# Attention and a mixture of experts on one core: the experts' split weights get two sets of buffers, the short block a second full stationary tile, and the planner a new table

## The chip, the cores and the metric

The kernel runs on one core of a Trainium2 chip. The metric is the device time of one execution in microseconds. Engines are called TensorE (PE; its weight loads are PEld), VectorE (DVE), ScalarE (ACT), GpSimd (POOL) and SyncE (SP, which issues DMAs); the DMA engines move data beside them. L1709 is line 1709 of the kernel before.

## The reference

The first part is attention with pooled queries over 8 batches and 8 heads of 1152 x 64; its output is laid out as 4608 tokens of 512 numbers. The second part is a mixture of 8 experts with a fixed capacity of 576 tokens each:

```python
logits = x @ w_gate                      # (4608, 8)
order = np.argsort(-logits.flatten())    # best pair of token and expert first
for idx in order:
    tok, e = idx // E, idx % E
    if assigned[tok] >= 0 or counts[e] >= cap: continue
    assigned[tok] = e; counts[e] += 1
    ...
for e in range(E):
    mask = assigned == e
    h = np.maximum(x[mask] @ w1[e], 0.0)   # w1[e] is 512 x 1024
    out[mask] = h @ w2[e]                  # w2[e] is 1024 x 512
```

## The kernel before, in words

Attention comes first. Its order of instructions is written out in a table of its own (class `Timed`, table `TIME`), and the change leaves that table alone. Behind it stands `experts`, which handles the eight experts in turn, in the order in which they fill up. For an expert k three functions add operations to one list:

- `route(k, ...)` finds by a search in rounds (L1282 to L1311, VectorE with small matmuls L1288 and L1297) which expert fills up next and which tokens it gets; its result is the table of indices `idx[k]`. The next expert's routing needs this one's result.
- `fetch(k, ...)` loads the raw 32-bit weights W1 and W2 (L1563, indirect DMAs from GpSimd's queue) and the rows of x (XG, L1568). For the first two experts TensorE transposes x (`by_pe`, L1509 to L1518); for the others VectorE transposes squares of 32 and SP moves them into place with 16 DMAs (`by_dve`, L1528, L1535), then ScalarE and GpSimd split them (L1547, L1549, L1553). All matmuls work on 16-bit floats: each operand is split into a high half (rounded) and a low half (what the rounding left). So that the halves keep their range, the weights are scaled by a power of two, which comes from the sum of their squares: ScalarE squares W1 (L1587, tag `wq`) and W2 (L1609, tag `vq`) in four pieces each, small matmuls of one moving column add up the partitions (L1596, tag `ws`, and L1615, tag `vt`), and VectorE makes the scale (L1600, L1619). Then 16 pieces of the weights are split (tags `wh` and `vh` for the high halves on ScalarE, `wl` and `vl` for the low ones on GpSimd, L1663). For nearly all pieces ScalarE does a pair of operations: it scales the 32-bit piece in place (L1653) and copies it to the 16-bit high half (L1657); GpSimd then subtracts the high half from the scaled piece.
- `ffn(k, ...)` does the two products. The first (L1679, tag `mm`): 8 blocks of 128 hidden columns in two parts of 256 and 320 tokens, 12 matmuls each into PSUM tiles `ph`. Of each part ScalarE makes a pair (tag `re`): Relu in place in PSUM (L1684), then a copy to the high half HH (L1685); VectorE subtracts to get the low half HL (L1689, L1691). HH and HL lie side by side in one tile HX. The second product (L1709, tag `m2`): 5 blocks of tokens into `po`, four of 128 tokens and a short one of 64. A full block takes 24 matmuls of 512 moving columns, three for each of 8 pieces z: HH with W2H, HH with W2L, HL with W2H. The short block takes 16: one whose 128 stationary columns are the 64 of HH and the 64 of HL together, with W2H (L1706), and one whose stationary columns are the 64 of HH alone, with W2L. ScalarE takes a block out of PSUM (L1714, or L1717 and VectorE's L1719 for the short one) and GpSimd scatters it to the output (L1724, function `put`).

What sets the order: `Order.emit` is a planner in the program that builds the kernel. It knows for each operation the engine, a duration in ns (the number behind the engine's name in `od.add`), what it reads and writes by keys, and costs of handing over between engines (`EOWN`, `EWAIT`, and `switch` for TensorE between small and large matmuls). It plays the list through; where several operations of an engine are ready it takes the one with the smallest `(-first, t + lead)`, t being 10 per expert and a little more for later stages, `lead` coming from the table ELEAD by tag. From ELATE comes a delay in ns by which an operation's users are held back in the plan. The kernel's instructions are then issued in the planned order; each engine works its own list in that order and waits at an instruction until what it needs is there. The keys of the halves, `("W1H", z, y)` and so on, are the same for all experts, as there is one set of buffers W1h, W1l, W2H, W2L (and one of the raw weights W1, W2): an expert's halves can be written only when the matmuls of the expert before that read that piece are done.

Of the kernel before, what the change touches and what calls it, by code (L numbers as in the profile page):

```python
# [51 lines left out]
class Order:  # L52
# [15 lines left out]
    def add(self, t, eng, dur, fn, r=(), w=(), late=0, first=0, tag=None, kind=0, lock=None, k=None):  # L68
# [5 lines left out]
        late = late + self.late.get(tag, 0)  # L74
        pri = t + self.lead.get(tag, 0) + (self.lead.get(f"{tag}.{k}", 0) if k is not None else 0)
# [492 lines left out]
def attention(ctx, tc, top, kb, sx, kt, qt, v, wg, x_dram, L, npair=NPAIR):  # L568
# [483 lines left out]
    for n in range(1, npair, 2):  # L1052
# [8 lines left out]
        else:  # L1061
# [16 lines left out]
ELEAD = {"ar": 4.9, "be": 51.6, "bo": 2.8, "cl": 28.5, "cmp": 29.1, "dv": 1.5, "dw": -46.1, "dx": -41.8,  # L1078
# [5 lines left out]
ELATE = {"ar": -300, "bo": -300, "cl": -300, "cmp": 150, "dv": 1900, "dw": 750, "dx": 1500, "fa": -150, "fl": -300,  # L1084
# [4 lines left out]


def experts(ctx, tc, top, kb, sx, x_dram, L, w1, w2, out, C):
# [91 lines left out]
    W1h, W1l = one([128, 4, F], F16, "W1h"), one([128, 4, F], F16, "W1l")  # L1183
# [6 lines left out]
    W2H, W2L = one([128, 8, DM], F16, "W2H"), one([128, 8, DM], F16, "W2L")  # L1190
# [331 lines left out]
    def by_dve(k, t):  # L1522
# [8 lines left out]
        for s in range(4):  # L1531
# [14 lines left out]
            def high(src=src, cols=cols):  # L1546
                nc.scalar.activation(src, src, AF.Copy, scale=xs)  # L1547
                for o, c in cols(Xh):
                    nc.scalar.copy(o, src[:, :, c])  # L1549
# [240 lines left out]
```

## Time and profile before

| | us |
|---|---|
| median of the runs (lowest to highest of 3) | 1340.38 (1337.77 to 1343.58) |
| the profiled execution | 1334.67 |
| its span in the trace | 1332.9 |
| TensorE busy in the span (matmuls) | 1244.5 (93%) |
| VectorE | 1052.7 (79%) |
| ScalarE | 993.6 (75%) |
| GpSimd | 761.6 (57%) |

The page of the profile also gives the busy share of each engine in 40 slices of the span:

```profile
PE   7899999999999999999999997789899999999796
DVE  8999999999999999999999966888786777643020
ACT  4578777877887777787787660679887888897681
POOL 5275566656657556665665660365575565656351
PEclk7799999999999999999999998989999999999898
DMA  5755764665666566476465400442543534333301
```

Each digit is the busy share of a slice of 33.3 us in tenths; PEclk is the clock granted to TensorE in tenths of full speed. The experts begin near the 25th slice. Matmuls are pipelined: a matmul's duration holds the time until its result is out, so starts of neighbours, not durations, tell what one costs.

### The profile page before, as it was taken

Reading aid. Unit: us, or ns where it says so; the run is one execution under the profiler, and the core shown is the slowest. Engines: PE = TensorE matmul, PEld = TensorE weight load, DVE = VectorE, ACT = ScalarE, POOL = GpSimd, SP = SyncE. Lnnn points to the kernel's source line nnn. Section 1 sums busy time; section 2 is a strip of 40 time slices with the busy share of each in tenths; the row PEclk is TensorE's granted clock in tenths of the full one; section 3 lists DMA queues with packets and bytes.
Section 4 is the critical chain, followed back from the end, with each engine's and each line's share of the span. In section 5 each row is a group of like instructions: output and inputs, shape, how many; then the busy total and the mean of one; then the engine's idle time right before and its main releaser. Section 6 shows DMA issues by size and latency. Waiting matters only on the chain.

```text
span 1332.9 us, 39667 instructions
## 1 busy us (share of the span) xinstructions
PE 1244.5 (93%) x15483; PEld 884.1 (66%) x15483; DVE 1052.7 (79%) x2662; ACT 993.6 (75%) x2299; POOL 761.6 (57%) x757
## 2 busy tenths in 40 slices
PE   7899999999999999999999997789899999999796
PEld 4577787778778777777777775555554646556362
DVE  8999999999999999999999966888786777643020
ACT  4578777877887777787787660679887888897681
POOL 5275566656657556665665660365575565656351
PEclk7799999999999999999999998989999999999898
DMA  5755764665666566476465400442543534333301
GB/s 156 172 144 131 173 165 119 170 155 128 166 151 156 130 159 161 117 187 158 113 172 132 107 15 19 163 169 90 154 134 107 197 103 147 123 127 119 116 21 36
DMA packets 123545, 175.29 MB, mean 132 GB/s; under 512 B 49500, under 2 KB 86364, under 8 KB 121180
## 3 DMA queue, kind: packets, MB, share of 16 engines
q1 hardware_dynamic: 114876, 120.29, 35.6%
q0 software_dynamic: 8336, 52.44, 11.4%
q8 instruction: 121, 1.98, 0.7%
q14 instruction: 68, 0.56, 0.1%
q10 hardware_dynamic: 144, 0.02, 0.0%
HBM read 99.63 MB, written 18.87 MB: 89 GB/s over the span
## 4 chain that ended last, share of the span: by engine, by line
PE 58%; DVE 15%; ACT 13%; issue 7%; DMA 4%; SPq 1%; POOL 1%; ACTq 0%; POOLq 0%; DVEq 0%
PE av L890 16%; PE mt L770 9%; PE sc L873 6%; PE po L1709 6%; PE sc L874 5%; PE ph L1679 5%; DVE MX L797 4%; ACT W L1653 3%; PE kb L873 3%; PE kb L874 3%; DVE PM L880 2%; ACT WQ L1609 2%; DMA XG<-XB 1%; ACT W2H L1657 1%; ACT HX L1685 1%
## 5 line engine op out<-in xcount | busy, mean ns | idle before, releaser
L880 POOL TENSOR_TENSOR PM<-P 128x576 f16<-128x576 f32 x413 | 474.0, 1175 | 312.8 <-ACT P L877 263.0
L797 DVE TENSOR_REDUCE MX<-mt 128x2 f32<-128x768 f32 (+1 forms) x443 | 399.4, 921 | 39.6 <-PE mt L770 36.5
L877 ACT ACTIVATE P<-sc 128x288 f32<-128x288 f32 x768 | 296.5, 413 | 139.2 <-PE sc L874 127.6
L890 PEld LDWEIGHTS <-P 128*128 128x128 bf16 x5760 | 297.2, 98 | 28.1 <-issue 1.3
L890 PE MATMUL av<-V,P 128*128 128x65 f16 (+1 forms) x5760 | 305.8, 193 | 0.0
L890 PE MATMUL av<-V,PM 128*128 128x65 f16 x2880 | 296.4, 195 | 0.0
L890 PEld LDWEIGHTS <-PM 128*128 128x128 f16 x2880 | 265.4, 97 | 0.0
L874 PE MATMUL sc<-QB,KB 66*128 66x288 f16 (+1 forms) x768 | 216.7, 288 | 2.0 <-DMA QB<-AU 1.4
L873 PE MATMUL sc<-QA,KA 128*128 128x288 f16 x768 | 215.4, 286 | 1.7 <-ACT P L877 1.4
L770 PE MATMUL mt<-KH,BD 128*128 128x384 f16 x837 | 200.6, 326 | 10.4 <-DVE MX L797 4.5
L877 ACT ACTIVATE P<-kb 128x288 f32<-128x288 f32 x384 | 158.2, 412 | 32.9 <-PE kb L874 31.4
L1709 PE MATMUL po<-W2H,HX 128*128 128x512 f16 x512 | 165.8, 392 | 3.5 <-ACT OT L1714 3.5
L1709 PEld LDWEIGHTS <-HX 128*128 128x128 f16 (+1 forms) x832 | 77.5, 100 | 112.7 <-issue 46.7
L1679 PE MATMUL ph<-Xh,W1h 128*128 128x320 f16 (+1 forms) x512 | 147.9, 289 | 2.7 <-ACT Xh L1516 1.5
L874 PEld LDWEIGHTS <-KB 66*128 66x128 f16 (+1 forms) x1152 | 112.1, 97 | 56.3 <-issue 16.9
L1679 PE MATMUL ph<-Xl,W1h 128*128 128x320 f16 (+1 forms) x512 | 147.8, 289 | 0.6 <-DVE Xl L1518 0.6
L1679 PE MATMUL ph<-Xh,W1l 128*128 128x320 f16 (+1 forms) x512 | 147.8, 289 | 0.0
L873 PEld LDWEIGHTS <-KA 128*128 128x128 f16 x1152 | 112.9, 98 | 49.6 <-issue 15.8
L880 DVE TENSOR_TENSOR PM<-P 128x576 f16<-128x576 f32 x163 | 127.7, 793 | 6.8 <-ACT P L877 5.8
L1709 PE MATMUL po<-W2L,HX 128*128 128x512 f16 (+1 forms) x320 | 126.4, 395 | 0.0
L1663 POOL TENSOR_TENSOR W1l<-W,W1h 128x512 f16<-128x512 f32 x62 | 71.7, 1157 | 93.7 <-ACT W1h L1657 58.8
L1679 PEld LDWEIGHTS <-W1h 128*128 128x128 f16 x1024 | 99.9, 99 | 32.8 <-issue 5.7
(271 smaller groups left out, 2174.1 us busy)
## 6 DMA issues: line engine op xcount, KB each, us to landing
QD<-in_qt_dram SPq DMA_DIRECT2D x32, 576.0 KB
KD<-in_kt_dram SPq DMA_DIRECT2D x64, 288.0 KB
VD<-in_v_dram SPq DMA_DIRECT2D x32, 576.0 KB
QA<-QH SPq DMA_DIRECT2D x128, 72.0 KB
KA<-KH SPq DMA_DIRECT2D x64, 144.0 KB
KB<-KH SPq DMA_DIRECT2D x64, 144.0 KB
KA<-KL SPq DMA_DIRECT2D x64, 144.0 KB
x_dram<-X SPq DMA_DIRECT2D x16, 576.0 KB
```

The lines of the kernel that those rows point to most:

```text
L770: nc.tensor.matmul(out, BD[i][:, j], KH[i][:, ks], start=True, stop=True)
L797: od.add(t, "DVE", d, lambda: nc.vector.tensor_reduce(dst, src, axis=AX.X, op=OP.max), r=[mk], w=[("MX", i, j, c) for j, c in what], tag=" ...
L873: nc.tensor.matmul(c[:, :288], KA[i][:, s, ks], QA[i][:, s, qs], start=True, stop=False)
L874: nc.tensor.matmul(c[:, :288], KB[i][:kr, s, ks], QB[i][:kr, s, qs], start=False, stop=True)
L877: od.add(g + 0.1 + 0.01 * t, "ACT", 293, lambda c=c, qs=qs: nc.scalar.activation(p[:, qs], c[:, :288], AF.Exp, scale=1.0 / UNIT), r=[ck], ...
L880: od.add(g + 0.2, en, dur, lock=1, fn=lambda: eng.tensor_tensor(pm, p, hi, op=OP.subtract), r=[("P32", g % NP, 0), ("P32", g % NP, 1)], w= ...
L890: nc.tensor.matmul(out, w[:, qs], v, start=kb == 0 and j == 0 and y == 0, stop=kb == NKB - 1 and y == 2, skip_group_check=True)
L1609: od.add(t + 0.5, "ACT", 960, lambda z=z: nc.scalar.activation(WQ, W2.rearrange("p a b -> p (a b)")[:, 1024 * z:1024 * z + 1024], AF.Squar ...
L1653: nc.scalar.activation(a, a, AF.Copy, scale=by)
L1663: eng.tensor_tensor(o, a, b, op=OP.subtract), r=[key] + sr + [(nm + "H", z, y)], w=[(nm + "L", z, y)], first=first, lock=1, tag="wl" if nm ...
L1679: nc.tensor.matmul(p, a[:, d, fs], b[:, d, qs], start=z == 0, stop=z == 11)
L1709: nc.tensor.matmul(o[:n], a[:, z, q0:q0 + n], b[:, z], start=z == 0 and y == 0, stop=z == 7, skip_group_check=True)
```

## The change

1. The halves of both weights get two sets of buffers, used in turn by even and odd experts (`W1h[k % 2]` and so on), and the keys carry the set. The raw weights W1 and W2 keep one buffer each.
2. In the short block the second kind of matmul takes all 128 stationary columns (HH and HL together) with W2L, where it took the 64 of HH. So HL times W2L is added as well.
3. ScalarE's pairs are turned round: it first writes the 16-bit high half from the unscaled piece, with the scale (or Relu) in the same operation, and then scales the 32-bit piece in place, again with the scale, where the second operation of the pair was a plain copy before. This holds for weights, for x of `by_dve` and for Relu.
4. The planner gets new figures: some durations, `switch` 10 in place of 95, and new tables ELEAD and ELATE, which have an entry by tag and one more by tag and expert (`tag@k`); both are added. The tags `vq`, `vt` and `vw` had no entry before.
5. A drain of GpSimd is put before the last expert's third scatter.

```diff
-        late = late + self.late.get(tag, 0)
-        pri = t + self.lead.get(tag, 0) + (self.lead.get(f"{tag}.{k}", 0) if k is not None else 0)
+        late = late + self.late.get(tag, 0) + self.late.get(f"{tag}@{int(t // 10)}", 0)
+        pri = t + self.lead.get(tag, 0) + self.lead.get(f"{tag}@{int(t // 10)}", 0)
...
-         "tb": 145.1, "tk": 562.6, "tr": -103.1, "vh": 54.6, "vl": 44.3, "wh": 45.9, "wi": -101.8, "wl": 86.7,
-         "wq": 49.7, "ws": 12.4, "xb": -54.5, "xh": -50.5, "xl": 43.1, "xr": -50.0}
...
+         "vl@5": 36.3, "vl@6": 47.2, "vl@7": -42.3, "vq": 137.3, "vq@0": -54.4, "vq@1": 77.4, "vq@2": 47.1,
+         "vq@3": -7.9, "vq@4": -6.3, "vq@5": 31.1, "vq@6": -136.3, "vq@7": 10.1, "vt": -75.2, "vt@0": 77.2,
...
+         "vw@6": 36.8, "vw@7": 21.2, "wh": 36.7, "wh@0": 6.4, "wh@1": 10.3, "wh@2": -96.9, "wh@3": -96.7,
...
+         "wl@7": 11.3, "wq": 157.6, "wq@0": 31.4, "wq@1": -50.2, "wq@2": 39.1, "wq@3": -0.7, "wq@4": -79.5,
...
+         "vl@1": -150, "vl@2": 400, "vl@3": 700, "vl@4": -300, "vl@5": 50, "vl@6": -300, "vl@7": 2150, "vq":
+         2900, "vq@0": -200, "vq@1": -250, "vq@2": -300, "vq@3": -300, "vq@4": -300, "vq@5": -250, "vq@6": 650,
...
-    od.OWN, od.WAIT, od.switch = EOWN, EWAIT, 95
+    od.OWN, od.WAIT, od.switch = EOWN, EWAIT, 10
...
-    W1h, W1l = one([128, 4, F], F16, "W1h"), one([128, 4, F], F16, "W1l")
+    W1h, W1l = ([one([128, 4, F], F16, f"{x}{i}") for i in range(2)] for x in ("W1h", "W1l"))
...
-    W2H, W2L = one([128, 8, DM], F16, "W2H"), one([128, 8, DM], F16, "W2L")
+    W2H, W2L = ([one([128, 8, DM], F16, f"{x}{i}") for i in range(2)] for x in ("W2H", "W2L"))
...
-            od.add(t + 0.5, "ACT", 960, lambda z=z: nc.scalar.activation(
+            od.add(t + 0.5, "ACT", 1050, lambda z=z: nc.scalar.activation(
...
                     def high(o=hi[p], a=raw[p], by=by, on_dve=on_dve):
+                        nc.scalar.activation(o, a, AF.Copy, scale=by)
                         if not on_dve:
                             nc.scalar.activation(a, a, AF.Copy, scale=by)
-                        if on_dve:
-                            nc.scalar.activation(o, a, AF.Copy, scale=by)
-                        else:
-                            nc.scalar.copy(o, a)
-                    od.add(tt, "ACT", 515 if on_dve else 1080, high,
-                           r=[key] + sr, w=[(nm + "H", z, y)], first=first, tag="wh" if nm == "W1" else "vh")
+                    od.add(tt, "ACT", 535 if on_dve else 1075, high,
+                           r=[key] + sr, w=[(nm + "H", k % 2, z, y)], first=first, tag="wh" if nm == "W1" else "vh")
...
                 def relu(qs=qs, f=f, p=p):
+                    nc.scalar.activation(HH[:, f, qs], p, AF.Relu, scale=HS)
                     nc.scalar.activation(p, p, AF.Relu, scale=HS)
-                    nc.scalar.copy(HH[:, f, qs], p)
...
-                pairs = ((HH, W2H), (HH, W2L), (HL, W2H)) if c < 4 else ((HX, W2H), (HH, W2L))
+                w2h, w2l = W2H[k % 2], W2L[k % 2]
+                pairs = ((HH, w2h), (HH, w2l), (HL, w2h)) if c < 4 else ((HX, w2h), (HX, w2l))
...
-                            nc.tensor.matmul(o, a[:, z, 512:640], b[:, z], start=z == 0, stop=z == 7, skip_group_check=True)
+                            nc.tensor.matmul(o, a[:, z, 512:640], b[:, z], start=z == 0 and y == 0, stop=z == 7 and y == 1,
+                                             skip_group_check=True)
...
             def put(c=c, n=n, ob=ob):
+                if (k, c) == (E - 1, 2):
+                    nc.gpsimd.drain()
                 nc.gpsimd.memset(spacer, 0.0)
```

## Rows read from the trace of the kernel before

**Rows 1.** Busy time by stretch: us, then each engine, TensorE's clock, DMA share, GB/s.

```profile
0.00:848.00 848.00, 806.66 (x12497) 627.01 (x12498) 777.06 (x1553) 614.76 (x1562) 497.32 (x467) 0.98 0.55 139
...
1048.40:1106.70 58.30, 54.87 (x389) 32.14 (x387) 41.39 (x167) 48.85 (x96) 35.57 (x40) 0.97 0.42 134
```

**Rows 2.** Waits from 848 us on: us in total, times, longest.

```profile
PE rt L1615 <- ACT WQ L1609: 16.2, 11, 2.3
...
PE po L1709 <- ACT OT L1714: 3.5, 1, 3.5
```

**Rows 3.** Waits of ScalarE in one period, 1048.4 to 1106.7 us.

```profile
ACT OT L1714 <- PE po L1709: 4.7, 1, 4.7
ACT ph L1684 <- PE ph L1679: 2.9, 5, 0.9
```

**Rows 4.** Timeline of TensorE, end of a second product: start, duration, instruction.

```profile
1087.46 0.38 PE L1709 MATMUL po<-W2L,HX 128*128 128x512 f16 x1
...
1088.11 0.38 PE L1709 MATMUL po<-W2L,HX 128*128 128x512 f16 x1
...
1090.85 0.38 PE L1706 MATMUL po<-W2H,HX 128*128 128x512 f16 x1
1091.16 0.40 PE L1709 MATMUL po<-W2L,HX 128*64 128x512 f16 x1
...
1096.09 0.28 PE L1679 MATMUL ph<-Xh,W1h 128*128 128x256 f16 x1
```

**Rows 5.** Timeline of TensorE, first and last of four like waits.

```profile
1022.49 0.16 PE L1615 MATMUL rt<-VS,mones 128*128 128x1 bf16 x1 [2.18 <-ACT WQ L1609]
...
1196.07 0.16 PE L1615 MATMUL rt<-VS,mones 128*128 128x1 bf16 x1 [2.08 <-ACT WQ L1609]
```

**Rows 6.** TensorE by stretches of 5 us: busy, clock, DMA share, GB/s.

```profile
865.00:870.00 5.00, 0.86 (x10) 0.93 0.00 0
...
1080.00:1085.00 5.00, 4.26 (x19) 0.66 0.00 0
...
1250.00:1255.00 5.00, 2.29 (x8) 0.50 0.14 52
```

**Rows 7.** Timeline ahead of the last expert: GpSimd, SP's queue, ScalarE.

```profile
1222.97 0.97 POOL L1563 DMA_INDIRECT W<-in_w_dram,widx  x1
...
1223.66 20.74 SPq L1535 DMA_DIRECT2D XG<-XB  x16
...
1241.04 0.83 ACT L1547 ACTIVATE XG<-XG,sx 128x640 f32<-128x640 f32 x1 [6.95 <-DMA XG<-XB]
```

**Rows 8.** Timeline of ScalarE: Relu pairs (their first operations), then a weight pair.

```profile
1055.15 0.38 ACT L1684 ACTIVATE ph<-ph 128x256 f32<-128x256 f32 x1
...
1055.83 0.43 ACT L1684 ACTIVATE ph<-ph 128x320 f32<-128x320 f32 x1
...
1056.62 0.38 ACT L1684 ACTIVATE ph<-ph 128x256 f32<-128x256 f32 x1
...
1064.33 0.72 ACT L1653 ACTIVATE W<-W,we 128x512 f32<-128x512 f32 x1
1065.09 0.62 ACT L1657 CAST W1h<-W 128x512 f16<-128x512 f32 x1
1065.61 0.72 ACT L1653 ACTIVATE W<-W,we 128x512 f32<-128x512 f32 x1
```

**Rows 9.** Timeline of VectorE: L1282 twice, with what follows it.

```profile
1064.48 0.82 DVE L1282 SCALAR_TENSOR_TENSOR GE<-kb,base,nib 128x576 bf16<-128x576 f32 x1
1065.22 0.14 DVE L1605 TENSOR_SCALAR we<-we 128x1 int32<-128x1 int32 x1
...
1067.40 0.82 DVE L1282 SCALAR_TENSOR_TENSOR GE<-kb,base,nib 128x576 bf16<-128x576 f32 x1
1068.25 0.26 DVE L1311 TENSOR_SCALAR kb<-kb,base 128x36 f32<-128x36 f32 x1
```

**Rows 10.** Timeline of GpSimd, a scatter of the last expert.

```profile
1312.12 0.96 POOL L1724 DMA_INDIRECT out_dram<-OT,idx  x1 [4.14 <-ACT OT L1714]
```

More of the change, by code (lines that the diff above doesn't have):

```diff
@@ L1546, in high @@
             def high(src=src, cols=cols):
+                for o, c in cols(Xh):
+                    nc.scalar.activation(o, src[:, :, c], AF.Copy, scale=xs)
                 nc.scalar.activation(src, src, AF.Copy, scale=xs)
-                for o, c in cols(Xh):
-                    nc.scalar.copy(o, src[:, :, c])
             def low(src=src, cols=cols, eng=None):
@@ L1554, in by_dve @@
             xf = [("XF", s, q) for q in range(4)]
-            od.add(t + 0.35, "ACT", 1350 if nc_ == 5 else 1050, high, r=xf + xg, w=hk, tag="xh")
+            od.add(t + 0.35, "ACT", 1400 if nc_ == 5 else 1075, high, r=xf + xg, w=hk, tag="xh")
             en, eng, d = ("DVE", V, 800 if nc_ == 5 else 602) if s >= LT["xp"] else ("POOL", nc.gpsimd, 1700)
@@ L1631, in fetch @@
         wk = [("wf", k, 0), ("wf", k, 1)] + [("we", h) for h in range(2)] * (not k)
-        od.add(t + 0.55, "DVE", 290 if k else 650, weigh2, r=["rv"] + wk, w=["ve", "vb", ("wo", k)], tag="vw", lock=0)
+        od.add(t + 0.55, "DVE", 580 if k else 1000, weigh2, r=["rv"] + wk, w=["ve", "vb", ("wo", k)], tag="vw", lock=0)
         for z in range(4):
@@ L1636, in fetch @@
                     fs = slice(256 * z, 256 * z + 256)
-                    raw, hi, lo = W1[:, z // 2, :, 256 * (z % 2):256 * (z % 2) + 256], W1h[:, :, fs], W1l[:, :, fs]
+                    raw, hi, lo = W1[:, z // 2, :, 256 * (z % 2):256 * (z % 2) + 256], W1h[k % 2][:, :, fs], W1l[k % 2][:, :, fs]
                     tt, key = t + 0.4, ("W1", z // 2)
@@ L1641, in fetch @@
                     fs = slice(2 * z, 2 * z + 2)
-                    raw, hi, lo = W2[:, fs], W2H[:, fs], W2L[:, fs]
+                    raw, hi, lo = W2[:, fs], W2H[k % 2][:, fs], W2L[k % 2][:, fs]
                     tt, key = t + 0.6, "W2"
@@ L1662, in fetch @@
                            eng.scalar_tensor_tensor(o, a, by, b, op0=OP.mult, op1=OP.subtract) if on_dve else
-                           eng.tensor_tensor(o, a, b, op=OP.subtract), r=[key] + sr + [(nm + "H", z, y)], w=[(nm + "L", z, y)], first=first, lock=1, tag="wl" if nm == "W1" else "vl")
+                           eng.tensor_tensor(o, a, b, op=OP.subtract), r=[key] + sr + [(nm + "H", k % 2, z, y)], w=[(nm + "L", k % 2, z, y)], first=first, lock=1, tag="wl" if nm == "W1" else "vl")
     scat = []
@@ L1676, in ffn @@
                 xk = [y for x in ("XH", "XL") for y in xkeys(x, 256 * hf, 256 * hf + qn)]
[L1677 removed]
+                for z, (d, a, b) in enumerate((d, a, b) for d in range(4) for a, b in ((W1h[k % 2], Xh), (W1h[k % 2], Xl), (W1l[k % 2], Xh))):
                     def mm(fs=fs, qs=qs, p=p, z=z, d=d, a=a, b=b):
                         nc.tensor.matmul(p, a[:, d, fs], b[:, d, qs], start=z == 0, stop=z == 11)
[L1680 removed]
+                    od.add(t + 0.5, "PE", 138 if hf else 111, mm, r=xk + [(x, k % 2, f // 2, y) for x in ("W1H", "W1L") for y in range(2)],
                            w=[("ph", f % 2, hf)], tag="mm")
                 def relu(qs=qs, f=f, p=p):
+                    nc.scalar.activation(HH[:, f, qs], p, AF.Relu, scale=HS)
                     nc.scalar.activation(p, p, AF.Relu, scale=HS)
[L1685 removed]
                 def rest(hf=hf, qs=qs, f=f, p=p):
@@ L1692, in ffn @@
                 pk, hk = [("ph", f % 2, hf)], [("HH", f, hf)]
-                od.add(t + 0.5, "ACT", 690 if hf else 590, relu, r=pk, w=hk, tag="re")
+                od.add(t + 0.5, "ACT", 670 if hf else 560, relu, r=pk, w=hk, tag="re")
                 od.add(t + 0.5, "DVE", 470 if hf else 335, rest, r=pk + hk, w=[("HL", f, hf)], tag="rs")
@@ L1710, in mm2 @@
                                              skip_group_check=True)
-                    od.add(t + 0.7, "PE", 216, mm2, r=[("HH", z, 0), ("HH", z, 1), ("HL", z, 0), ("HL", z, 1), ("W2H", z // 2, z % 2), ("W2L", z // 2, z % 2)],
+                    od.add(t + 0.7, "PE", 216, mm2, r=[("HH", z, 0), ("HH", z, 1), ("HL", z, 0), ("HL", z, 1), ("W2H", k % 2, z // 2, z % 2), ("W2L", k % 2, z // 2, z % 2)],
                            w=[("po", c % 2)], tag="m2")
             if c < 4:
-                od.add(t + 0.7, "ACT", 480, lambda n=n, o=o, ob=ob: nc.scalar.activation(OT[ob][:n], o[:n], AF.Copy, scale=wo[k][:n]),
+                od.add(t + 0.7, "ACT", 570, lambda n=n, o=o, ob=ob: nc.scalar.activation(OT[ob][:n], o[:n], AF.Copy, scale=wo[k][:n]),
                        r=[("po", c % 2), ("wo", k)], w=[("OT", ob)], tag="ot")
             else:
-                od.add(t + 0.7, "ACT", 480, lambda o=o: nc.scalar.activation(O64, o[64:], AF.Copy, scale=wo[k][64:]),
+                od.add(t + 0.7, "ACT", 570, lambda o=o: nc.scalar.activation(O64, o[64:], AF.Copy, scale=wo[k][64:]),
                        r=[("po", c % 2), ("wo", k)], w=["O64"], tag="ot")
```

10 lines of the change are left out of this document (4 added, 6 removed), and 110 rows, old and new, of tables (ELATE, ELEAD).

## The prediction

> **What bounds the kernel now.** I read the busy time of the engines by stage first. The profiled execution took 1334.67 us, 1.77 more than its span of 1332.9; it lies 5.71 under the median of the runs shown, 1340.38. Attention and the first expert's routing fill the first 848 us [rows 1]; the change leaves that code's order alone, so the sum is made over the 485 us behind it. There the middle experts repeat with a period of 58.3 us, the third stretch of [rows 1]. In it TensorE is marked busy for 54.9 us and ScalarE for 48.9. No other engine comes near (VectorE 41.4, GpSimd 35.6).
>
> The view of waits comes second, since a matmul that overlaps its neighbour looks busy all the time. The reader is to see which wait of TensorE is dear: over all experts L1615 waited 16.2 us in 11 waits for ScalarE's squares of W2, and one matmul of the second product waited 3.5 us for a result to leave PSUM [rows 2]. L1615 is a matmul of one column that nobody needs soon; it was put too early in TensorE's list, and what stands behind it waits too. Third, ScalarE's own waits in one period: 4.7 us once, 2.9 us in five, all for TensorE [rows 3]. So it is occupied for 58.3 - 7.6 = 50.7 us, nearly as much as TensorE. The 4.7 us lie where an expert's second product still reads W2H and W2L: all of W1 is split, and W2 may not be.
>
> Fourth, matmul by matmul: in blocks 0 to 3 two W2L matmuls with two others between them start at 1087.46 and 1088.11, so 0.216 us for one. The short block's 16, from 1090.85 to the 1096.09 of what follows, take 5.24 us, 0.33 each, though each streams the same 512 columns. What differs is that every second one has 64 stationary columns [rows 4].
>
> **The change part by part.**
>
> *Short block.* It removes 8 matmuls of 64 stationary columns per expert and adds 8 of 128, the form that stands in blocks 0 to 3. At 0.216 us the 16 take 3.45 us: 1.79 us less per expert, 14.3 us for eight. Bounds: 0 if TensorE only waits instead, 14.3 if it is the limit; the last expert's 1.8 us count at any rate, since there nothing else runs. I take 14.3, because the block is followed at once by the next expert's first matmul [rows 4].
>
> *The early L1615.* The planner's new figures let W2's squares (tag vq) last 1050 ns instead of 960 and hold their users back by a further 2.6 us in most experts, where the old table had nothing; four long waits of one shape, a period apart, run from 2.18 us in the first to 2.08 in the last [rows 5], the longest 2.3 [rows 2]. Around the second, TensorE's mean clock over the 5 us from 1080 is 0.66 [rows 6], a mix of the half level of 1.2 GHz and the full 2.4: 0.34 x 5 = 1.7 us lost, of which I put 0.4 inside the wait itself and 1.3 behind it. So 2.3 + 1.3 = 3.6 us for each, 14.4 us for four. Bounds: 0 if the small matmul is early again, 14.4; I take 14.4, as the new margin is longer than the wait.
>
> *The first expert.* From 865 to 870 TensorE works 0.86 us of 5 [rows 6]: ScalarE squares W2 before it splits the second half of W1. The new leads put vq (82.9) behind that splitting (wh, 43.1); before it was 0 against 45.9, smaller first. Four squares moved behind give 4 us; but W1's own squares (wq, 189) now stand behind vq too. Bounds 0 and 5; I take the middle, 2.5.
>
> *The last expert's hole.* At 1222.97 GpSimd fetched W1 and W2 together, and 16 moves of XG were issued by SP over the 20.7 us from 1223.66; ScalarE stood 6.95 us at 1241.04 for them [rows 7]. Results and squares queued behind it, TensorE went without work and its clock to 0.50 [rows 6]. An estimate from [rows 2, 6]: 3.5 us of wait for the result, some 5 of the 7.3 that are left of L1615's 16.2 without the four above, and 2.8 of half clock in the 5.5 us that follow; 11.3 us. Two sets let W2 be split during the second product, so its raw buffer comes free and its fetch can start apart from the moves; but the new order isn't bound to do so. Bounds 0 and 11.3; I take half, 5.6.
>
> *Two sets of halves.* No instruction is added. The wait that goes is the 4.7 us of ScalarE [rows 3]: it can split W2 there. What is late next is TensorE itself. Its period after is 58.3 - 1.8 - 3.6 = 52.9 us; ScalarE's 50.7 us of work fit into that only if little of it waits. I charge 3 us over all experts for new waits, between 0 and the 2.2 us per full expert of the rival below. The tiles behind lie at other addresses, at nothing: no row shows an address that matters.
>
> *Pairs turned round.* In a weight pair the in-place scaling starts at 1064.33, the copy 0.76 later (it reads what was scaled), the next pair at 1065.61: 1.28 us, the last 0.10 of the 0.62 overlapping [rows 8]. A Relu pair takes 0.68 (256 columns) or 0.79 (320). Turned, the second operation overwrites what the first reads and needs nothing from it. If ScalarE doesn't hold it back, both overlap: 2 x (0.72 - 0.10) = 1.24 us for weights, since the second now has a scale from memory and lasts 0.72 where the copy lasted 0.62, and 0.55 and 0.65 for Relu (0.14 less). VectorE does hold such a pair back: L1311, which overwrites what L1282 reads, starts 0.85 us after it, a stranger (L1605) 0.74 after it [rows 9]. Held so, a weight pair takes 0.76 + 0.61 = 1.37 and Relu as before. For 16 weight pairs, four pairs of x and 16 of Relu per expert, ScalarE gets between 2.2 + 0.8 = 3.0 us less and 1.8 us more. For the sum I take nothing: what hides it is ScalarE's slack of 52.9 - 50.7 us. If the pairs are held that cover is gone, which is a rival.
>
> The Trainium skill, "ScalarE: Activation LUTs" (section What ACT_TABLE_LOAD costs), says that each per-partition scale operand adds about 93 ns and that ScalarE's operations back to back overlap by about 93 ns. The first half speaks against the change and agrees with 0.72 against 0.62 [rows 8]; by the second a weight pair would take about 1.25 us, an estimate from that page, whereas VectorE's held pair makes 1.37.
>
> *The drain* on GpSimd stands ahead of the third last scatter, where GpSimd waits 4.14 us for its block anyway [rows 10]. No row shows a drain; between 0 and the 0.96 us of the scatter itself, all covered; behind it only that scatter and two more are queued.
>
> **Sum.** 14.3 + 14.4 + 2.5 + 5.6 - 3.0 = 33.8 us. The profiled execution would take 1300.9 us; the median moves by the same: 1340.38 - 33.8 = 1306.6, say 1306 us.
>
> **Rivals.**
>
> ScalarE becomes the limit. If the pair is held back it needs 50.7 + 1.8 = 52.5 us per expert, and the 2.9 us in which Relu waits for matmuls [rows 3] come on top, 55.4 less what can be filled: some 2.2 over TensorE's period in four full experts and less in the others, about 10 in all: 1316 us. For it: the rows of VectorE. Against: ScalarE need not do as VectorE does, and the two sets let weight work fill the 2.9.
>
> Only the short block pays. The new list takes the early L1615 away and puts as many waits elsewhere, since the planner knows the chip only by its table: 1340.4 - 14.3 = 1326 us. For it: today's waits are all of a planner that was wrong by 1 to 2 us. Against: the margins now cover these. If even the short block's time turns into waiting, the change does nothing: 1340.
>
> Slower: the fetches collide with the moves in many experts. Two sets let both fetches go out together, as at 1222.97, and every such hole costs 11.3 us. The forecast counts half a hole. With three more than today's it is 33.8 - 5.6 - 33.9, level with before; from the fourth the kernel is slower, at 1340.4 - 33.8 + 5.6 + 45.2 = 1357 us. For it: SP's moves of an expert and both weights share the same DMA engines, and the two collided in the one case seen. Against: it was one of six experts whose rows of x are moved by SP; the weights of the next expert can't be fetched before its routing is done.
>
> **How the numbers follow.** Forecast 0.62 (its own range 1290 to 1316); ScalarE the limit 0.15 (1316); only the short block 0.11 (1326); nothing gained 0.05 (1340); collisions 0.07 (1357). A run of this kernel tells about 0.5% (6.7 us) from no change. Faster than 1333.7: 0.62 + 0.15 + 0.10 = 0.87; within: 0.01 + 0.05 = 0.06; slower: 0.07. The range ends below where all waits of the sum go, no new ones come (1306 - 3 - 2.5 - 5.7 = 1295) and the smaller waits of the second and third expert go too, up to 10 us: 1285. It ends above behind the short-block case, at 1330, so that no more than the last two cases are left out.
>
> **What would show it.** Right: the short block's 16 matmuls in about 3.5 us; no L1615 wait over 1 us on TensorE; a middle period of 52 to 54 us; W2H written while an earlier expert's second product runs; the second of a turned pair starting 0.62 us (0.27 for Relu) behind the first. Wrong step by step: 0.76 there (held); ScalarE without idle time beside a waiting TensorE; moves of XG that end over 15 us after their issue; a first stretch that isn't 848 us.

## The result, and the profile after

The changed kernel takes 1322.05 us (median; 1319.86 to 1323.47), the kernel before beside it 1340.4: ratio 0.9861, 95% interval [0.9834, 0.9887]. A second comparison gave 0.9845 [0.9817, 0.9873]. That is 18 to 21 us less where 34 were forecast; the range held, about half of the gain came. The kernel before took 1331 us beside some of the kernels below and 1345 beside others, so only ratios are compared from one group of runs to the next; a thousandth is 1.34 us.

The profiled execution took 1323.47 us (span 1321.7; before 1334.67 and 1332.9). Two rows of the page's slices, after:

```profile
PE   7899999999999999999999997697888899999898
...
ACT  4578777777877887877777761396897988899971
```

From the 25th slice on ScalarE shows six nines, before two; TensorE's first eight digits there are 7, 6, 9, 7 and four eights, before 7, 7, 8, 9, 8 and three nines. Where the 11.2 us of span went, by the ends of the short blocks (the start of VectorE's last operation on each):

| stretch | before | after | difference | after, without the drain |
|---|---|---|---|---|
| to the first matmul of the experts | 848.0 | 853.2 | +5.2 | 852.3 |
| first expert, to the end of its short block | 75.7 | 73.9 | -1.8 | 67.7 |
| to the end of the fourth expert | 177.0 | 185.3 | +8.3 | 180.6 |
| to the end of the eighth | 221.5 | 204.7 | -16.8 | 202.2 |
| to the end of the span | 10.7 | 4.6 | -6.1 | 10.7 |

The last column is the profile of the changed kernel without its drain (a run below). Its engines work the same lists in the same order up to the drain, yet its last computation starts 14.4 us earlier. The profile after holds waits that nothing in the program releases (the view of waits calls them remote), and TensorE's search matmul waits 4.0 us behind the largest of them:

```profile
DVE dg L1391 <- remote: 4.8, 1, 4.8
```

From 830 us on such waits stand in five profiles (the changed kernel both times, scalings first, all pairs back, the short block at 64 columns again) and in none of the other nine. What causes them no run shows. So the pair of profiles before and after isn't like with like: by it over half of the gain lies behind the last computation, by the last column 19.5 us are gained ahead of it, and the loss from the second expert to the fourth is 3.6 us rather than 8.3. Busy time by stretch, after: the first stretch, one middle period and all experts (columns as in [rows 1]):

```profile
0.00:853.20 853.20, 808.70 (x12506) 628.00 (x12507) 780.54 (x1567) 618.49 (x1567) 498.18 (x468) 0.98 0.54 140
1054.20:1112.40 58.20, 53.36 (x392) 32.64 (x393) 42.65 (x177) 51.34 (x98) 37.50 (x42) 0.94 0.45 139
848.00:1317.30 469.30, 421.59 (x2988) 258.01 (x2988) 273.79 (x1114) 384.19 (x739) 263.95 (x291) 0.96 0.38 123
```

The last of these before:

```profile
848.00:1322.00 474.00, 437.88 (x2986) 257.06 (x2985) 274.87 (x1109) 378.71 (x738) 263.35 (x290) 0.96 0.36 120
```

The reader is to see two things. TensorE is busy 16 us less, ScalarE 5.5 us more. And the middle period is still 58.2 us, as in [rows 1], where 52 to 54 were expected. Without the drain it is 55.5, at a clock of 1.00 in place of 0.94, so 2.7 us of it don't come from the change:

```profile
1045.00:1100.50 55.50, 51.46 (x392) 31.74 (x393) 42.63 (x176) 51.01 (x98) 37.60 (x42) 1.00 0.46 145
```

The three largest waits of TensorE from 848 us on, after, and the one that was the largest in [rows 2]:

```profile
PE po L1807 <- ACT OT L1812: 10.3, 7, 3.2
PE rt L1397 <- DVE red L1393: 9.2, 6, 4.0
PE ph L1776 <- DVE HX L1786: 6.1, 7, 3.0
...
PE rt L1715 <- ACT WQ L1709: 0.2, 1, 0.2
```

The early matmul of one column (now L1715) waits 0.2 us instead of 16.2: the forecast's largest repair was made. But all waits of TensorE behind 848 us add up to 46.9 us, before to 36.4. What is new are waits for results that ScalarE takes out of PSUM late (12.8 us with L1803's; before 3.5), for the halves of Relu (HX, 7.9; before 1.0), and for VectorE's search (19.4; before 13.4). In the profile without the drain the sum is 38.0 us, and these three are 13.6, 8.3 and 15.6: most of what the search added belongs to the waits called remote, the other two are the change's.

ScalarE's pairs, after: a Relu pair of 320 columns and the next one, then a weight pair and the start of the next:

```profile
1119.68 0.42 ACT L1781 ACTIVATE HX<-ph 128x320 f16<-128x320 f32 x1
1120.00 0.43 ACT L1782 ACTIVATE ph<-ph 128x320 f32<-128x320 f32 x1
1120.36 0.37 ACT L1781 ACTIVATE HX<-ph 128x256 f16<-128x256 f32 x1
...
1129.21 0.72 ACT L1752 ACTIVATE W1h<-W,we 128x512 f16<-128x512 f32 x1
1130.02 0.72 ACT L1754 ACTIVATE W<-W,we 128x512 f32<-128x512 f32 x1
1130.65 0.71 ACT L1752 ACTIVATE W1h<-W,we 128x512 f16<-128x512 f32 x1
```

The second operation of the Relu pair starts 0.32 us behind the first, that is 0.10 before its end; the pair takes 0.68 where it took 0.79 [rows 8]. The second of the weight pair starts 0.81 behind, 0.09 after the first has ended: it is held back, and the pair takes 1.44 us where it took 1.28. In the trace's records it carries a wait on ScalarE's own semaphore, and the second of a Relu pair carries none. In 109 of 124 weight pairs it also waits on a semaphore of GpSimd, with one more instruction in between, and starts 0.80 us behind the first; in the other 15 it is 0.74, as in all of the kernel before with its pairs turned (below). The mean pair takes 1.43 us. The Trainium skill, "ScalarE: Activation LUTs" (section What ACT_TABLE_LOAD costs), has ScalarE's operations back to back overlap by about 93 ns; Relu's pair agrees (0.10 us). The pair that overwrites what its first operation reads in SBUF doesn't overlap at all, and there the measurement decides.

The end of the last short block, after: both kinds at 128 columns and 0.216 us each (0.22 and 0.21 by turns), 16 in about 3.5 us, where [rows 4] shows 0.33:

```profile
1315.53 0.38 PE L1803 MATMUL po<-W2L,HX 128*128 128x512 f16 x1
1315.75 0.38 PE L1803 MATMUL po<-W2H,HX 128*128 128x512 f16 x1
1315.96 0.38 PE L1803 MATMUL po<-W2L,HX 128*128 128x512 f16 x1
```

And GpSimd at the end, after. The drain stands ahead of the first of these rows; the last scatter of the kernel before started at 1323.22 and its span ended 9.7 us later, here 3.6 us later:

```profile
1312.53 0.09 POOL L1823 MEMSET spacer<- 1x1 f32 x1 [7.82 <-issue]
1313.28 0.96 POOL L1824 DMA_INDIRECT out_dram<-OT,idx  x1 [0.67 <-issue]
...
1318.12 0.90 POOL L1824 DMA_INDIRECT out_dram<-OT,idx  x1 [2.52 <-DVE OT L1817]
```

The program ends with drains of GpSimd of its own. Before (L1786), then after (L1886, and L1822 for the added one); the three numbers are the shortest, middle and longest duration in ns:

```profile
L1786 POOLq DRAIN  x3: 40/102/9132, 1323.0 to 1332.6; - x3
```

```profile
L1886 POOLq DRAIN  x3: 46/102/2977, 1317.9 to 1321.4; - x3
L1822 POOLq DRAIN  x1: 8950/8950/8950, 1303.5 to 1303.5; - x1
```

The long closing drain lasts 9.13 us in the six kernels without the added one and 2.98 to 3.00 in the eight with it. The added one lasts 8.95 us, at a time when TensorE still works.

### The profile page after: what moved, and what is told of

Read it like the earlier page. It is cut to its first block, busy times and chain, and to the rows that moved or that the text cites. A ratio compares the mean times of both kernels' runs of the same rounds, so it can differ in the third digit from the quotient of the medians.

```text
span 1321.7 us, 39674 instructions
## 1 busy us (share of the span) xinstructions
PE 1228.9 (93%) x15483; PEld 885.0 (67%) x15483; DVE 1049.9 (79%) x2662; ACT 998.6 (76%) x2299; POOL 759.9 (57%) x757
## 4 chain that ended last, share of the span: by engine, by line
PE 62%; DVE 14%; ACT 12%; issue 7%; DMA 3%; POOL 1%; another core or an unknown queue 1%; SPq 0%; POOLq 0%; ACTq 0%; DVEq 0%
PE av L890 17%; PE mt L770 9%; PE ph L1776 8%; PE sc L873 6%; PE sc L874 6%; PE po L1807 5%; DVE MX L797 4%; PE kb L873 3%; ACT W L1754 3%; PE kb L874 3%; DVE PM L880 2%; ACT W2H L1752 2%; ACT W1h L1752 1%; ACT HX L1781 1%; ACT ph L1782 1%
## 5 line engine op out<-in xcount | busy, mean ns | idle before, releaser
L797 DVE TENSOR_REDUCE MX<-mt 128x2 f32<-128x768 f32 (+1 forms) x443 | 399.6, 922 | 39.7 <-PE mt L770 36.4
L1807 PE MATMUL po<-W2H,HX 128*128 128x512 f16 x512 | 152.1, 382 | 10.3 <-ACT OT L1812 10.3
L1807 PEld LDWEIGHTS <-HX 128*128 128x128 f16 x768 | 72.0, 98 | 95.3 <-issue 21.5
L1776 PE MATMUL ph<-Xh,W1h 128*128 128x320 f16 (+1 forms) x512 | 125.5, 294 | 10.5 <-DVE HX L1786 6.1
L1776 PE MATMUL ph<-Xl,W1h 128*128 128x320 f16 (+1 forms) x512 | 124.0, 293 | 0.3 <-DVE Xl L1618 0.3
L1776 PE MATMUL ph<-Xh,W1l 128*128 128x320 f16 (+1 forms) x512 | 123.5, 293 | 0.0
L1786 DVE TENSOR_TENSOR HX<-ph,HX 128x256 f16<-128x256 f32 x128 | 52.9, 418 | 75.6 <-ACT ph L1782 63.3
```

Of the source, the lines that this page charges most:

```text
L797: od.add(t, "DVE", d, lambda: nc.vector.tensor_reduce(dst, src, axis=AX.X, op=OP.max), r=[mk], w=[("MX", i, j, c) for j, c in what], tag=" ...
L1776: nc.tensor.matmul(p, a[:, d, fs], b[:, d, qs], start=z == 0, stop=z == 11)
L1786: V.tensor_tensor(HL[:, f, 64 + 256 * hf:320 + 256 * hf], p[:, :256], h[:, :256], op=OP.subtract)
L1807: nc.tensor.matmul(o[:n], a[:, z, q0:q0 + n], b[:, z], start=z == 0 and y == 0, stop=z == 7, skip_group_check=True)
```

## The experiments

**The drain alone.** The kernel before with:

```diff
+                if (k, c) == (E - 1, 2):
+                    nc.gpsimd.drain()
                 nc.gpsimd.memset(spacer, 0.0)
```

> The kernel before with the drain of GpSimd alone added ahead of the last expert's third scatter; nothing else differs. In the two profiled executions the last scatter of the kernel before is followed by 9.7 us until the span ends (1323.22 to 1332.9), that of the changed kernel by 3.6 us (1318.12 to 1321.7). Theory A, the forecast's: the drain costs and gives nothing, 0 us (ratio 1.000), and those 6.1 us are either not a lasting difference or come from something else in the list. Theory B: the drain has GpSimd settle its outstanding DMAs ahead of the last scatters, so the program's end needs less; then this kernel takes about 6 us less than before (ratio 0.9955), and its last scatter is followed by about 3.6 us. [...]

Measured: ratio 0.9956 [0.9941, 0.9971], 5.9 us less; theory B. GpSimd's rows:

```profile
1313.06 0.09 POOL L1725 MEMSET spacer<- 1x1 f32 x1 [7.82 <-issue]
...
1320.55 0.90 POOL L1726 DMA_INDIRECT out_dram<-OT,idx  x1 [4.42 <-DVE OT L1719]
```

It stands 7.82 us at the drain, waiting for nothing that the profile shows, and two scatters queue behind it; but TensorE still works for 5.7 us, so nobody waits. The span ends at 1324.1, 3.6 us behind the start of the last scatter.

**A memset in the drain's place.**

```diff
+                if (k, c) == (E - 1, 2):
+                    nc.gpsimd.memset(spacer, 0.0)
                 nc.gpsimd.memset(spacer, 0.0)
```

> The kernel before with a second memset of the small spacer in the place where the changed kernel has its drain. It tells what of the drain matters, if anything does: if any added instruction moves GpSimd's code so that its end is fetched earlier, this takes the 6 us off the end as well (last scatter followed by about 3.6 us); if only a drain does it, the end stays at about 9.7 us and the time is that of the kernel before; by the forecast's theory, 0 us in either case.

Measured: 1.0004 [0.9995, 1.0013]. Its last scatter starts at 1320.62 and the span ends at 1330.3, 9.7 us later:

```profile
1320.62 0.90 POOL L1726 DMA_INDIRECT out_dram<-OT,idx  x1 [4.82 <-DVE OT L1719]
```

So it is the drain, not one more instruction. In all profiles taken here the time from VectorE's last operation to the end is 10.7 us in the six kernels without it and 4.5 or 4.6 us in the eight with it. The trace shows where the 6.1 us go: out of the closing drain, into the added one, which is covered. What either of them settles no row shows.

**The changed kernel without the drain.** The two lines taken out.

> The changed kernel without its drain. By the run of the kernel before with only the drain (ratio 0.9956), the drain gives 5.9 us at the end of the program: this kernel would take 5.9 us more than the changed one (ratio to before 0.9905) with some 9.7 us between the last scatter and the end of the span instead of 3.6. By the forecast's theory (the drain costs and gives nothing) 0.986.

Measured: 0.9883 [0.9858, 0.9908]. Against 0.9861 and 0.9845 that is 3 to 5 us more, and the intervals overlap: by time alone inconclusive. Its end is 10.7 us again, and its closing drain 9.13.

**The short block alone.** The kernel before with:

```diff
-                pairs = ... if c < 4 else ((HX, W2H), (HH, W2L))
+                pairs = ... if c < 4 else ((HX, W2H), (HX, W2L))
...
-  start=z == 0, stop=z == 7, skip_group_check=True)
+  start=z == 0 and y == 0, stop=z == 7 and y == 1, skip_group_check=True)
```

> The kernel before with the short block's second kind of matmul at 128 stationary columns, nothing else. The forecast's theory, TensorE as the limit of every expert: 16 matmuls take 3.5 us where they took 5.24, 14.3 us less over eight experts (ratio 0.9893). The rival, that time saved on TensorE turns into waiting for ScalarE (whose occupied time per expert is 50.7 us of a period of 58.3) or for VectorE's routing: between 1.8 us (the last expert alone, ratio 0.9987) and half of the forecast's. Before's other waits for ScalarE (the matmul of one column, 16.2 us in 11) would grow by what is lost.

Measured: 0.9959 [0.9944, 0.9974], 5.5 us less, 38% of the term. TensorE's busy time over the span fell by 13.2 us, nearly the 14.3 worked out (1244.5 to 1231.3). In the middle period from 1039.9 to 1097.5 it is 1.78 us less (54.77 to 52.99), but the period is only 0.6 us shorter. Its waits there, first before, then with the new short block:

```profile
PE rt L1288 <- DVE W L1275: 0.5, 1, 0.5
PE rt L1474 <- DVE idx L1433: 0.5, 1, 0.5
```

```profile
PE rt L1288 <- DVE W L1275: 1.3, 1, 1.3
PE rt L1474 <- DVE idx L1433: 0.8, 1, 0.8
```

1.1 of the 1.2 us that went missing stand here: the small matmuls of the next expert's search have fixed places in TensorE's list and wait for VectorE. In this period VectorE's search is late next. The wait for W2's squares didn't grow (16.3 us in 11).

**The pairs turned round alone.** The kernel before, same order, with all three pairs turned (weights shown; x and Relu alike):

```diff
+                        nc.scalar.activation(o, a, AF.Copy, scale=by)
                         if not on_dve:
                             nc.scalar.activation(a, a, AF.Copy, scale=by)
-                        if on_dve:
-                            nc.scalar.activation(o, a, AF.Copy, scale=by)
-                        else:
-                            nc.scalar.copy(o, a)
```

> The kernel before with ScalarE's pairs of weights, of x and of Relu turned round (the 16-bit half first, then the 32-bit operand in place), same order of instructions. The forecast's theory: 0 us, since TensorE is the limit and ScalarE's slack hides a difference either way; the second operation starts 0.62 us behind the first of a weight pair. The rival: the in-place operation is held back until the first has read its operand, 0.81 us as seen in the changed kernel, so a weight pair takes 1.43 us where it took 1.28 and ScalarE's work grows by 16 x 0.15 + 0.6 - 1.5 = 1.5 us per expert (Relu's pairs, which aren't held, give 1.5 back); where TensorE waits for ScalarE this reaches the end: 5 to 12 us slower (ratio 1.004 to 1.009).

Measured: 1.0021 [1.0007, 1.0034], 2.8 us slower; the rival's sign, about half of its lowest price (5 us). The pairs are held here too:

```profile
1065.32 0.71 ACT L1652 ACTIVATE W1h<-W,we 128x512 f16<-128x512 f32 x1
1066.06 0.72 ACT L1654 ACTIVATE W<-W,we 128x512 f32<-128x512 f32 x1
1066.68 0.71 ACT L1652 ACTIVATE W1h<-W,we 128x512 f16<-128x512 f32 x1
```

1.36 us (1.38 in the mean), within 0.01 of the forecast's "held" 1.37. ScalarE is late by that, and TensorE's wait for the squares grows:

```profile
PE rt L1615 <- ACT WQ L1609: 19.8, 14, 2.8
```

**Weights and x back, Relu still turned.** The changed kernel with:

```diff
+                nc.scalar.activation(src, src, AF.Copy, scale=xs)
                 for o, c in cols(Xh):
-                    nc.scalar.activation(o, src[:, :, c], AF.Copy, scale=xs)
-                nc.scalar.activation(src, src, AF.Copy, scale=xs)
+                    nc.scalar.copy(o, src[:, :, c])
...
-                        nc.scalar.activation(o, a, AF.Copy, scale=by)
                         if not on_dve:
                             nc.scalar.activation(a, a, AF.Copy, scale=by)
+                        if on_dve:
+                            nc.scalar.activation(o, a, AF.Copy, scale=by)
+                        else:
+                            nc.scalar.copy(o, a)
```

> The changed kernel with the pairs of weights and of x in the old order again (in-place scaling first, then a plain copy); Relu's pair stays turned, the order of instructions stays. The forecast's theory: ScalarE's slack hides the pairs, so the time is that of the changed kernel (ratio to before 0.986). Theory two: turned and held back (1.43 us for a weight pair where it took 1.28), ScalarE's work is on the chain that sets the end for part of the time, since TensorE now waits 12.8 us for results that ScalarE takes out of PSUM late; 128 pairs by 0.15 us and the pairs of x by 0.1 to 0.2 are 24 us of ScalarE's time, of which a quarter to a half would reach the end: 6 to 12 us less than the changed kernel (ratio to before 0.977 to 0.982), with those 12.8 us falling below 6.

Measured: 0.9695 [0.9681, 0.9708] (1290.36 us, the kernel before beside it 1330.65): 20 to 22 us less than the changed kernel, twice what theory two expected. The changed kernel without its drain, in the same comparison, took 1314.28 us; less the drain's 6.1 us that is 18 us more than here, and by the profiles the last computation starts 21.6 us earlier here. So the price is 18 to 22 us. Which part of it the weights have and which x, no run separates. The largest waits of TensorE from 848 us on, and a middle period:

```profile
PE po L1810 <- ACT OT L1815: 4.4, 5, 1.6
PE rt L1388 <- DVE CAPS L1577: 4.2, 2, 2.5
PE rt L1397 <- DVE red L1393: 3.6, 4, 2.1
PE ph L1779 <- DVE HX L1789: 3.1, 4, 1.9
```

```profile
1033.00:1086.00 53.00, 51.38 (x397) 31.97 (x396) 42.63 (x177) 48.87 (x98) 37.62 (x42) 1.00 0.51 152
```

53.0 us: the period that the forecast gave, 52.9 (55.5 in the changed kernel without its drain). All waits of TensorE add up to 23.0 us (38.0 there, 46.9 in the changed kernel), and what the lower clock took, worked out from windows of 5 us as the sum of 5 x (1 - clock), is 6.1 us (10.2 and 17.2). ScalarE's waits in that period are 3.2 us, so it is occupied for 49.8.

**All pairs back.** In the same kernel also:

```diff
-                    nc.scalar.activation(HH[:, f, qs], p, AF.Relu, scale=HS)
                     nc.scalar.activation(p, p, AF.Relu, scale=HS)
+                    nc.scalar.copy(HH[:, f, qs], p)
```

> The changed kernel with all three pairs (weights, x, Relu) in the old order: what the change would be without its third part. Against the kernel with only Relu turned (0.9695) ScalarE needs 8 x 0.08 + 8 x 0.11 = 1.5 us more per expert, as much as the held pairs cost in the changed kernel. If it is ScalarE's occupied time that sets the end, the price is the same, some 20 us: ratio 0.984. If it is the place of the work (Relu stands ahead of the second product, the weights beside it), Relu's order costs little: 0.970 to 0.974. The forecast's theory, pairs at nothing: 0.9695, and the sum that it gave without the pairs, 33.8 us, would be this kernel's gain (0.9747).

Measured: 0.9809 [0.9776, 0.9842]; Relu's turn is worth 15 us (interval about 5 either way). It was expected that ScalarE's occupied time sets the price: 20 us; or the place: 0 to 6. It lies nearer to the first. Against the changed kernel in the same comparison (0.9845) it is 5 us less, interval 6 either way: the third part of the change as a whole isn't told from nothing. Busy time from 848 us to the last matmuls (fourth number behind the comma: ScalarE), weights and x back, then all back, then the changed kernel in its second profile:

```profile
848.00:1281.00 433.00, 410.29 (x2982) 254.72 (x2982) 270.65 (x1103) 366.16 (x735) 261.32 (x289) 0.99 0.41 132
```

```profile
848.00:1312.00 464.00, 421.52 (x2986) 257.17 (x2984) 271.54 (x1110) 378.01 (x738) 263.06 (x291) 0.97 0.38 124
```

```profile
848.00:1316.00 468.00, 421.19 (x2982) 257.27 (x2982) 272.00 (x1107) 381.95 (x736) 262.74 (x290) 0.96 0.38 122
```

ScalarE's busy time is 11.9 us more with Relu back, and 15 us came out. The turned pairs of weights and x add 15.8 us busy, and with the gap in which the second operation is held 122 x 0.15 + 24 x 0.15 = 22 us occupied; 18 to 22 came out. Over these three kernels ScalarE's time reaches the end nearly one for one.

**Scalings first.** The changed kernel, x back, weights in groups of two pieces:

```diff
...
-                        nc.scalar.activation(o, a, AF.Copy, scale=by)
-                        if not on_dve:
-                            nc.scalar.activation(a, a, AF.Copy, scale=by)
+                        if on_dve:
+                            nc.scalar.activation(o, a, AF.Copy, scale=by)
+                            return
+                        if y == 0:
+                            for b in both:
+                                nc.scalar.activation(b, b, AF.Copy, scale=by)
+                        nc.scalar.copy(o, a)
```

> The changed kernel with the pairs of x in the old order, and with the weights' operations in the old direction but grouped by two pieces: first both in-place scalings, then the two plain copies, so that each copy's source was written one operation earlier and nothing need be waited for. An estimate from the timelines: 0.72 + 0.62 + 0.52 + 0.42 = 2.28 us for two pieces, where the old pairs take 2.56 and the turned ones 2.86. Theory two (ScalarE's time sets the end, and each us of it in an expert costs more than one): the grouping gives ScalarE 8 x 0.28 = 2.2 us less per expert than the kernel with old pairs (0.9695), hence 8 to 20 us less than that kernel, ratio 0.955 to 0.963. If TensorE's own list sets the end by now, which the 23 us of waits left in that kernel speak for (7 of them for ScalarE), at most 4 us less (0.9665); the forecast's theory, no difference to the changed kernel (0.986).

Measured: 0.9677 [0.9646, 0.9708], 2.4 us less than with the old pairs, not told from none. ScalarE did become faster: two pieces take 2.27 us from the first row to what follows the second, as estimated, and it is busy 355.8 us behind 848 (366.2). The time did not follow:

```profile
1112.90 1.34 ACT L1757 ACTIVATE W<-W,we 128x512 f32<-128x512 f32 x2
1114.14 1.12 ACT L1758 CAST W1h<-W 128x512 f16<-128x512 f32 x2
1115.17 0.43 ACT L1785 ACTIVATE HX<-ph 128x320 f16<-128x320 f32 x1
```

TensorE's waits for ScalarE are down to 2.5 us, those for VectorE are 24.5. With the old pairs ScalarE has thus stopped being the limit. That VectorE is the next is argued and not shown: in this profile VectorE itself stands 4.9 and 3.5 us on waits called remote, and with the old pairs, where there are none, TensorE's waits for it are 15.9 us.

**The short block at 64 columns again**, in the kernel with weights and x back (the short block's edit above, undone):

> The kernel with the pairs of weights and x in the old order (0.9695), with the short block's second kind of matmul at 64 stationary columns again. It tells what the short block is worth where ScalarE is not held up. The forecast's term, TensorE as the limit: 14.3 us more, ratio 0.980. As in the kernel before (where 5.4 us of the 14.3 came out, and the routing matmuls' waits for VectorE grew instead): 0.9735.

Measured: 0.9759 [0.9722, 0.9796]: the short block is worth 8.6 us there (some 5 either way), between the two expectations.

**Two sets alone.** The kernel before with the two sets of halves and keys that carry the set, old tables:

```diff
-    W2H, W2L = one([128, 8, DM], F16, "W2H"), one([128, 8, DM], F16, "W2L")
+    W2H, W2L = ([one([128, 8, DM], F16, f"{x}{i}") for i in range(2)] for x in ("W2H", "W2L"))
...
-  w=[(nm + "H", z, y)]
+  w=[(nm + "H", k % 2, z, y)]
```

> The kernel before with two sets of buffers for the halves and keys that carry the set; the planner's old tables, so its order differs only by the keys. The forecast's theory: ScalarE's wait of 4.7 us per middle expert goes, but TensorE's list, with the early matmul of one column, still sets the end: at most 3 us either way (ratio 0.998 to 1.002). The rival, that ScalarE's chain (weights, squares, results) sets half of each period: then 2 to 4.7 us go in each of four to six experts, 8 to 28 us (ratio 0.979 to 0.994).

Measured: 0.9925 [0.99, 0.995], 10 us less, within the rival's range. The keys alone change the planned order, and the wait for W2's squares halves without any new figure:

```profile
PE rt L1615 <- ACT WQ L1609: 8.2, 11, 1.0
```

By the stretches of the table above, its last four experts take 195.4 us (221.5 before) and the second to the fourth 191.2 (177.0). So the gain late and the loss early come with the two sets and the order that their keys make, before any new figure.

**The changed code with the old figures** (tables, durations, switch 95):

```diff
-    od.OWN, od.WAIT, od.switch = EOWN, EWAIT, 10
+    od.OWN, od.WAIT, od.switch = EOWN, EWAIT, 95
```

> The changed code (two sets, short block, turned pairs, drain) with the planner's old tables, durations and switch cost. From the runs of single parts: drain -5.9 us, short block -5.4, turned pairs +2.8, together -8.5 us, to which two sets add what they bring. If the new figures make the rest of the change's 18.4 us, this kernel stands at ratio 0.9936; if the two sets make it, at 0.986, and the new figures bring nothing. The early matmul of one column would be there again (14 to 20 us of waits on TensorE for ScalarE's squares).

Measured: 1.0001 [0.9992, 1.001]. Neither expectation held: the four edits alone sum to 18.6 us (5.9, 5.5 and 10.0 less 2.8) and give nothing together in the old order. So the new figures, with all the edits there, are worth the whole gain, 18 to 21 us; alone, in the code before, they weren't run. Waits for VectorE took the place:

```profile
PE rt L1615 <- ACT WQ L1609: 10.3, 12, 1.1
PE rt L1288 <- DVE W L1275: 8.4, 3, 3.8
PE ph L1676 <- DVE HX L1686: 6.5, 5, 2.7
```

Which of the edits undoes which wasn't separated. The trace shows a part: the turned weight pair takes 1.42 us in the mean here and 1.38 with one set, as 86 of its 124 second operations wait on GpSimd's semaphore too. Over 124 pairs that is 5 us of ScalarE's time.

**The changed kernel again**, beside the others:

> The changed kernel once more, beside the other kernels, as their common point on one chip. Its first comparison gave ratio 0.9861 to before; without its drain 0.9883 was measured. If the drain gives its 5.9 us here too, it stands at 0.984 (0.9883 less 0.0044), within the first interval; if the drain gives nothing in this order, at 0.988.

Measured: 0.9845 [0.9817, 0.9873], the value expected if the drain gives its 5.9 us here too; the interval doesn't exclude the other.

## Why the prediction was right in its range and half wrong in its sum

| term | forecast | measured |
|---|---|---|
| short block | -14.3 | -5.5 alone, -8.6 beside the new order |
| early matmul, first expert, last hole, two sets with their new waits | -19.5 | about -11, a remainder (all pairs back 25.6, less drain and short block) |
| pairs turned | 0 | about +5 (18 to 22 lost with weights and x, 15 won with Relu) |
| drain | 0 | -5.9 |
| sum | -33.8 | -18 to -21 |

*The step that failed* is "For the sum I take nothing: what hides it is ScalarE's slack of 52.9 - 50.7 us." The price was right for one set of buffers: held, a weight pair takes 1.37 us by the forecast and 1.38 in the mean of that run. With two sets it takes 1.43, as the second operation waits on GpSimd's semaphore too; the two parts of the change were priced apart. So the held pairs of weights and x take 3.0 us more in one expert (16 x 0.15 and four of x), more than the slack of 2.2. That slack was read a little short: ScalarE has a third wait in the period of [rows 3], so it is 2.8 us, still less than 3.0.

```profile
ACT O L1717 <- PE po L1709: 0.6, 1, 0.6
```

That an average slack can't be filled in a list with fixed places fits this, but is argued. Relu's pair was put in the same "held" case and isn't held; its gain paid for most of the loss. The rival "ScalarE becomes the limit", 1316 us, is nearest to what happened, 6 us dearer, and 9 without the drain, which it didn't count. Had the weights and x not been turned, the forecast of 1306 (0.9747) would have been passed (0.9695). Part of the 18 to 21 us is luck: 5.9 came from the drain and 15 from Relu's turn, both priced at nothing.

*Short block.* The price per matmul was right, 0.216 us. That the end follows TensorE's work was wrong: "I take 14.3, because the block is followed at once by the next expert's first matmul" left out VectorE's search, which was 0.6 us behind in the middle period.

*The early L1615.* The wait is gone, 0.2 us of 16.2. That it would come back elsewhere was priced at 3.0 us for everything; waits of 46.9 us in place of 36.4 are 26.5 us of new ones when L1615's 16 are taken off (17.6 by the profile without the drain).

*First expert.* Its hole is filled, but the new leads put search matmuls ahead: in the seven kernels with the old order the experts' first matmul starts at 847.5 us in the mean (845.0 to 849.8), in the seven with the new at 852.4 (850.6 to 854.0). The sign "a first stretch that isn't 848 us" was named against the forecast, and it came.

*Last hole.* The moves of XG took 14.0 us in place of 20.7 and ScalarE's wait of 6.95 us isn't there. It is gone with two sets alone as well, where the moves still take 19.6 us. This is part of the 16.8 us won in the last four experts, how much no run separates; the collisions of the slower rival weren't seen.

*Two sets.* ScalarE's wait for TensorE at the second product fell from 4.7 us to 1.3 in the middle period. What the forecast didn't see is how it acts alone: through the keys on the order, 10 us, won in the last four experts and partly lost again from the second to the fourth.

*Drain.* "No row shows a drain" held for the rows shown, not for the trace: the program's own closing drain of 9.13 us stood there, from the last scatter on, and wasn't asked about. The price of nothing missed that the end of the program is part of the time.

Not settled: why the edits cancel in the old order beyond the 5 us above, how much of the 11 us is margin for L1615, how much the last hole and how much the two sets, and what the waits called remote are.

## What to carry to other kernels

When two engines are occupied to within some per cent of a period, price every edit on both as if each were the limit: here 3 us per expert on the engine "with slack" cost 20 us in the end. Turn a pair so that its second operation doesn't overwrite what the first still reads, or put a stranger between (2.27 us for two pieces in place of 2.56), and look in the trace at the distance of starts before counting on overlap. Subtract the last computation's end from the span's end: what lies there is time too. Before two profiles are compared stretch by stretch, look in both for waits that nothing in the program releases.

## What was not expected of the hardware

A write in place behind a reader was held on ScalarE for SBUF operands (starts 0.73 to 0.82 us apart for 0.72 us of work), not for Relu's operands in PSUM (0.27 and 0.32 us apart for 0.38 and 0.42). In the records the first carries a wait on ScalarE's own semaphore and the second none; whether the engine would need that wait no run shows. A drain of GpSimd that began 18 to 20 us ahead of the end lasted 8.95 us and shortened the program's closing drain from 9.13 to 2.98 us, its end from 10.7 to 4.6. What the lower clock took from TensorE fell with its waits, though not in step: 17.1 us at 36.4 us of waits (before), 10.2 at 38.0 (changed, without the drain), 6.1 at 23.0 (weights and x back).
